# Windowed attention and a gated feed-forward on one core: the second layer of units 8 to 15 as seven half-size products

## The chip, the cores and the metric

The kernel runs on one core of one Trainium2 chip. The metric is device time in microseconds (us): the time of one execution of the program on the chip. The engines are TensorE (PE, with its weight loads as PEld), VectorE (DVE), ScalarE (ACT), GpSimd (POOL) and SyncE (SP), which here issues the DMA transfers.

## What is computed

```python
# q, k, v: 8 x 8 heads x 576 x 64
scores = q @ k.T / sqrt(64)          # heads 0-3: the last 32 positions; heads 4-7: every 4th of the last 128
attn   = softmax(where(mask, scores, -1e9))
x      = (attn @ v), heads side by side   # 4608 tokens x 512
h      = x @ w_in                     # 512 -> 2048
g      = h * tanh(softplus(h))        # Mish
out    = g @ w_out                    # 2048 -> 512
```

The weights come as 64-bit floats and everything is single precision. The kernel keeps that precision by splitting numbers into a high and a low half-precision part and multiplying high x high, high x low and low x high.

## The kernel before

The 4608 tokens are worked through in 16 units of 288 tokens (`HT`), each half of one batch entry. A unit has four pairs of heads: pairs 0 and 1 attend to a plain window, pairs 2 and 3 to the dilated one. Units 0 to 2 run the attention in fp32 with transposes on TensorE ("direct"); units 3 to 15 run it in split half precision, with transposes by DMA.

The order of everything is written out by hand in the list `ORDER`: each word is one step of one unit (or of a piece of the weights), and a step that yields is continued when its name comes again. The names that matter here: `wl`, `wm`, `ws`, `ww`, `wp` load a piece of the weights (512 KB transfers), take its magnitudes, find its scale, build single-precision words out of the 64-bit ones (`w_words`, L406 to L409: a shift, then two passes on VectorE) and split them (`w_split`). `pr` (`prep`) scales q, k and v of a unit: VectorE reduces the magnitudes of q, k and v (L306), a small product spreads the bound over the partitions (L313), and the split parts follow. `sp`, `sc`, `ex`, `tp`, `va`, `tx` are the scores of a pair, their maximum and subtraction, the exponentials, the transposes, the product with v and the transposes of x. `ff` (`ff1`, L862) is the first layer for 256 of the 2048 hidden columns, ending in Mish on ScalarE (L867). `gt` (`gate`, L883 and L885) splits a chunk of 512 hidden columns: ScalarE writes the high part, VectorE the low part. `fo` (`ff2`, L895) is a quarter of the second layer for one of four blocks of 128 outputs: 12 products (4 blocks of 128 of the contraction by three split terms). After the fourth quarter ScalarE scales the block out of PSUM (L909) and SyncE stores it. `kw` issues products of zeros (L924).

```python
seq = [(1, 0, k) for k in range(FPC)] + [(0, i, k) for k in range(FPC) for i in (1, 0)]
for n, (wi, gi, k) in enumerate(seq):
    nc.tensor.matmul(po[:, :HT], w2[:, e, j, wi, k * P:(k + 1) * P], d["g"][j][:, gi, k, :], ...)
```

PSUM is four tiles `b` of two banks; the digit behind "=" in the list says which one a step takes. Every product with a new weight block has its own weight load.

Of the kernel before, what the change touches and what calls it, by code (L numbers as in the profile page):

```python
# [10 lines left out]
F16 = mybir.dt.float16  # L11
BF16 = mybir.dt.bfloat16
F32 = mybir.dt.float32
I32 = mybir.dt.int32
I64 = mybir.dt.int64
# [10 lines left out]
SUM_EXP = 14  # L26
TINY = 2.0 ** -40
EXP_BITS = 0x7F800000
P_SCALE = 2.0 ** 14
G_SHIFT = 2.0 ** -14  # L30
# [19 lines left out]
tx1.0 wp0.1.1 ww0.2.0 ff0.1=3 tx1.3 wl1.3.0 tx1.2 ff0.1 tx1.3 wp0.2.1 tx1.2 tx1.3 ff1.0=1 wl1.2.0 sp2.3=2 ff1.1=0  # L50
wl1.3.1 gt0.3=0 ff0.1 ff1.0 fs1 pr2 ff1.2=3 ff1.1 ff1.2 gt0.3 sc2.3 wm1.3.0 gt0.0=1 wp0.2.0 ww1.3.0 wm1.2.0 ww1.3.0
wp0.2.0 ff1.0 pr2=1 ff1.1 tp2.0=0 pr2 wm1.3.1 ww1.3.1 gt0.0 sp2.1=1 tp2.0 ff0.2=0 ff0.2 ff1.2 ww1.3.1 wl1.2.1 cs2
ff1.6=3 ww1.2.0 ex2.3 sc2.1 ws1.3=2 ff1.6 wm1.2.1 ws1.3 ex2.1 ff0.2 ww1.2.1 ff1.3=2 ff1.3 ws1.2=1 ww1.2.0 ws1.2 ff1.3
gt1.0=2 tp2.3=0 sp2.2=2 wp1.3.1 wp1.3.1 tp2.3 wp1.2.0 gt1.1=3 gt1.0 ff1.6 ff1.4=1 ww1.2.1 gt1.1 ff1.4 ld3 pr3 ff0.3=0
ff0.3 ff1.5=3 wp1.2.0 ff0.3 va2.3=0 wp1.3.0 pr3 ff1.5 ff1.4 wp1.2.1 va2.3 wl1.0.0 ff1.7=1 ff1.7 va2.3 sc2.2 pr3
wl1.0.1 wp1.2.1 ff1.5 gt1.2=4 tp2.1=3 gt1.2 ff1.7 va2.0=0 tp2.1 wm1.0.0 ww1.0.0 wp1.3.0 va2.0 wl1.1.1 ex2.2 ff0.5=1
ff0.5 va2.0 ff0.4=3 ff0.4 pr3 tp2.2=2 wm1.0.1 wl1.1.0 fo1.2.0=0 fo1.2.1 ff0.4 ww1.0.1 ff0.5 tx2.0=3 tp2.2 tx2.0
ww1.0.0 tx2.0 tx2.3=1 tx2.3 wm1.1.0 va2.1=2 fo1.2.2 tx2.3 va2.2=3 ww1.0.1 va2.1 va2.1 va2.2 fo1.3.0 fo1.3.1 tx2.1=1
va2.2 pr3=2 wm1.1.1 fs2 gt0.1=5 tx2.1 tx2.2=3 ww1.1.0 fo1.3.2 tx2.2 tx2.2 tx2.2 tx2.1 pr3 ww1.1.1 ws1.0=2 fo0.2.0=3
gt0.1 ws1.0 tx2.1 gt1.3=6 wp1.0.0 ws1.1=1 fo0.2.1 gt0.2=7 ww1.1.1 wp1.0.1 ws1.1 ww1.1.0 wp1.0.0 wp1.1.1 fo0.3.0  # L60
wp1.1.0 wp1.1.1 ff2.1=2 wp1.1.0 ff2.0=1 wp1.0.1 gt1.3 ff2.0 ol xa3 ff2.1 ff2.0 pr3 ff2.1 gt0.2 pr3 pr3 pr3 pr3 fo0.3.1
# [921 lines left out]
```

## Time and profile before

| | |
|---|---|
| median of 3 runs | 902.95 us (902.22 to 905.34) |
| profiled execution | 906.53 us, its span 904.8 us |
| TensorE busy | 892.1 us (99%) |
| VectorE, ScalarE, GpSimd busy | 605.2, 569.0, 18.7 us |
| mean granted clock of TensorE | 0.992 of full speed |
| second layer (L895) | 392.9 us busy in 3072 products |
| first layer (L862) | 390.3 us busy in 3072 products |

An engine's busy time is the union of its instructions' spans. Products are pipelined: the span of one holds its way through the array, so neighbours overlap, and the pace of a group is read from the starts of the group and of the one behind it. In the timeline a row gives start, length, engine, line, operation, output and inputs, shape and count, and in brackets the idle time before it.

### The profile page before, as it was taken

To read this page: it belongs to the slowest core of one execution; us is meant where nothing else is said; L and a number is where in the kernel's file an instruction comes from. 1 tells how busy PE (TensorE), PEld (TensorE's weight loads), DVE (VectorE), ACT (ScalarE), POOL (GpSimd) and SP (SyncE) were. 2 spreads that over 40 slices of the span, in tenths; PEclk is the share of its full clock that TensorE was granted. 3 is DMA by queue.
4 is the path that set the end of the run, shared out by engine and by line. 5 is a ranking of instruction groups with operands and counts; after the bars stand their busy time and mean duration, and the time that the engine had idled before them with its cause. 6 is when DMAs were issued, how large, how long until landed. Compare 5 with 4: busy or idle time off the path is not lost.

```text
span 904.8 us, 21327 instructions
## 1 busy us (share of the span) xinstructions
PE 892.1 (99%) x9181; PEld 722.7 (80%) x9184; DVE 605.2 (67%) x893; ACT 569.0 (63%) x827; POOL 18.7 (2%) x92
## 2 busy tenths in 40 slices
PE   8989999999999999999999999999999999999998
PEld 7868888778878888888888888888888888888776
DVE  4888989798998867767487686878656453722120
ACT  4678887485865856867584765868546845553141
POOL 1000002100000000000000000000000000000000
PEclk9899999999999999999999999999999999999999
DMA  7863440235445544332524435264053132141010
GB/s 241 233 244 107 141 144 12 86 95 119 120 119 127 105 77 124 86 70 72 115 56 109 80 72 116 61 133 99 16 105 96 28 63 50 33 71 29 7 34 27
DMA packets 161711, 84.20 MB, mean 93 GB/s; under 512 B 127312, under 2 KB 157520, under 8 KB 161616
## 3 DMA queue, kind: packets, MB, share of 16 engines
q1 hardware_dynamic: 161616, 82.84, 38.5%
q8 instruction: 72, 1.18, 0.5%
q14 instruction: 23, 0.19, 0.1%
HBM read 49.02 MB, written 9.44 MB: 65 GB/s over the span
## 4 chain that ended last, share of the span: by engine, by line
PE 92%; DVE 3%; SPq 2%; DMA 2%; issue 0%; ACT 0%; DVEq 0%; ACTq 0%
PE b L895 42%; PE b L862 40%; PE b L768 4%; PE b L620 3%; PE b L762 2%; PE b L924 1%; DMA raw<-in_w_out 1%; DVE w L422 1%; SPq L469 1%; DMA vn<-in_v 1%; SPq L471 0%; DVE raw L409 0%; PE b L739 0%; PE b L376 0%; DVE raw L408 0%
## 5 line engine op out<-in xcount | busy, mean ns | idle before, releaser
L895 PE MATMUL b<-g,w 128*128 128x288 f16 x3072 | 392.9, 286 | 0.0
L862 PE MATMUL b<-x,w 128*128 128x288 f16 x3072 | 390.3, 286 | 0.5 <-ACT pp L748 0.5
L862 PEld LDWEIGHTS <-w 128*128 128x128 f16 x3072 | 298.1, 98 | 75.8 <-issue 0.7
L895 PEld LDWEIGHTS <-w 128*128 128x128 f16 x3072 | 296.2, 98 | 74.1
L867 ACT ACTIVATE hm<-b,fs 128x576 f32<-128x576 f32 x128 | 93.1, 738 | 130.8 <-PE b L862 128.4
L885 DVE SCALAR_TENSOR_TENSOR g<-hm,sg,g 128x1152 f16<-128x1152 f32 x64 | 89.4, 1409 | 65.5 <-ACT g L883 65.5
L909 ACT ACTIVATE y<-b,fo 128x288 f32<-128x288 f32 x60 | 43.3, 736 | 62.9 <-PE b L895 55.8
L883 ACT ACTIVATE g<-hm,sg 128x1152 f16<-128x1152 f32 x64 | 79.0, 1243 | 3.7 <-PE b L895 3.4
L782 DVE RECIPROCAL rec<-den 72x8 f32<-72x8 f32 (+1 forms) x64 | 12.0, 188 | 73.0 <-ACT den L778 68.4
L691 ACT ACTIVATE sb<-sb,ln_p 96x768 f32<-96x768 f32 (+3 forms) x52 | 46.3, 895 | 14.6 <-DVE sb L652 14.3
L652 DVE TENSOR_TENSOR sb<-sb,nm 96x512 f32<-96x512 f32 (+4 forms) x64 | 49.2, 768 | 2.2
L650 DVE TENSOR_REDUCE nm<-sb 96x4 f32<-96x512 f32 (+4 forms) x64 | 48.8, 763 | 1.8
L783 DVE TENSOR_TENSOR xs<-b,rec 72x512 f32<-72x512 f32 (+1 forms) x64 | 39.7, 620 | 6.3
L867 ACT ACT_TABLE_LOAD x33 | 42.3, 1283 | 0.6
L644 DVE SCALAR_TENSOR_TENSOR sb<-b,sc,m_r 96x768 f32<-96x768 f32 (+1 forms) x26 | 25.4, 977 | 21.1 <-PE b L620 21.1
L691 ACT ACT_TABLE_LOAD x30 | 38.5, 1283 | 0.5
L532 ACT ACTIVATE qn<-qn,s 128x1152 f32<-128x1152 f32 x13 | 16.3, 1252 | 35.4 <-DVE s L302 35.4
L644 DVE SCALAR_TENSOR_TENSOR sb<-b,sc,m_d 72x832 f32<-72x832 f32 (+1 forms) x26 | 24.8, 954 | 19.1 <-PE b L620 19.1
L778 ACT ACTIVATE den<-b 96x6 f32<-96x6 f32 (+1 forms) x52 | 8.8, 170 | 40.0 <-PE b L768 38.9
L620 PEld LDWEIGHTS <-q 64*72 64x72 f16 (+1 forms) x1092 | 27.2, 116 | 6.4 <-issue 5.5
L729 DVE TENSOR_TENSOR p<-sb,p 96x768 f16<-96x768 f32 (+3 forms) x35 | 31.1, 894 | 0.0
L620 PE MATMUL b<-k,q 64*72 64x104 f16 (+3 forms) x1092 | 30.9, 210 | 0.0
(139 smaller groups left out, 822.1 us busy)
## 6 DMA issues: line engine op xcount, KB each, us to landing
qn<-in_qT SPq DMA_DIRECT2D x16, 576.0 KB
out_T<-y SPq DMA_DIRECT2D x64, 144.0 KB
raw<-in_w_in SPq DMA_DIRECT2D x16, 512.0 KB
raw<-in_w_out SPq DMA_DIRECT2D x16, 512.0 KB
vn<-in_v SPq DMA_DIRECT2D x48, 128.0 KB
vdn<-in_vd SPq DMA_DIRECT2D x32, 104.0 KB
knd<-in_kdT SPq DMA_DIRECT2D x16, 208.0 KB
knp<-in_kT SPq DMA_DIRECT2D x8, 320.0 KB
```

Of the source, the lines that this page charges most:

```text
L620: nc.tensor.matmul(o, q, k, start=start, stop=stop, skip_group_check=True)
L644: nc.vector.scalar_tensor_tensor(args[0], args[1], d["sc"][:nq], args[2], ALU.mult, ALU.add)
L650: nc.vector.tensor_reduce(nm[:nq, :, j:j + n], x, axis=AX.X, op=ALU.max, negate=True)
L652: nc.vector.tensor_tensor(blocked(sb, c0, n, w), x, nm[:nq, :, j:j + n].unsqueeze(3).broadcast_to([nq, 2, n, w]), op=ALU.add)
L691: nc.scalar.activation(x, x, AF.Exp, bias=ln_p[:nq])
L783: nc.vector.tensor_tensor(xs[:nq, :nb].rearrange("p j (h e) -> p h j e", h=2), avv[:, :, :, :D], rc.unsqueeze(3).broadcast_to([nq, 2, nb, ...
L862: nc.tensor.matmul(ph[:, h, :HT], w1[j][:, c, wi, k * P:(k + 1) * P], x_of(d, xi, c), start=(n == 0), stop=(n == len(seq) - 1))
L867: nc.scalar.activation(d["m"][j][:, k0:k0 + 2], ph[:, :, :HT], AF.Mish, scale=d["fs"][:, j:j + 1])
L883: nc.scalar.activation(g[:, 0], m, AF.Identity, scale=sg)
L885: nc.vector.scalar_tensor_tensor(g[:, 1], m, sg, g[:, 0], ALU.mult, ALU.subtract)
L895: nc.tensor.matmul(po[:, :HT], w2[:, e, j, wi, k * P:(k + 1) * P], d["g"][j][:, gi, k, :], start=(j == 0 and n == 0), stop=(j == NCH - 1 a ...
L909: nc.scalar.activation(o, src, AF.Identity, scale=fo)
```

## The change

The second layer of units 8 to 15 (`SEVENS`) is no longer one product of 512 outputs x 2048 hidden columns x 288 tokens but a Strassen scheme of Winograd's form: both factors and the result are cut into 2 x 2 quarters, and seven products of half the size in each direction are formed. Four of the weights' quarters enter as they are, three sums of weights are formed once (`w_sums`, in small steps while units 3 to 8 run) and kept in half-precision pairs; four sums of a unit's hidden values are formed in place for each half of the contraction (`gate_sums`), and seven quarters are split into parts (`gate_of`). For the sums all quarters must share one scale, so `rescale` brings the output weights to one scale, and the gates of all chunks use one factor (`g_1`, `sg` of width 1).

The three accumulators x, y, z of a unit lie side by side in one PSUM tile, and are read while later products still add to them; the last unit has them in three tiles. The outputs are stored as two blocks of 256 rows.

```diff
+    def gate_of(u, p, n):
...
+            src = m[:, :, :, :HF] if n in (0, 2) else m[:, :, :, HF:]
+        nc.scalar.activation(hi, src, AF.Identity, scale=sg)
+        yield
+        nc.vector.scalar_tensor_tensor(lo, src, sg, hi, ALU.mult, ALU.subtract)
+
+    def gate_sums(u, p):
+
+        b11, b12, b21, b22 = quarters(U[u]["m"][p])
+        for a, b, op in ((b22, b12, ALU.subtract), (b12, b11, ALU.subtract), (b11, b22, ALU.add), (b21, b11, ALU.subtract)):
+            nc.vector.tensor_tensor(a, a, b, op=op)
+            yield
+
+    PRODUCTS = (("11", 0, 0, 0), ("12", 0, 1, 2), (0, 3, 0, 1), (1, 2, 0, 0), (2, 3, 1, 0), (3, 1, 0, 1), ("22", 2, 1, 0))
+
+    def product(u, n, p):
...
+        acc = [d["po"][acc][:, e, acc * HF:(acc + 1) * HF] for e in range(2)]
...
+        for e in range(2):
+            for q, (wi, gi, k) in enumerate(seq):
+                nc.tensor.matmul(acc[e], left(l, e, p, wi)[:, k * P:(k + 1) * P], right(gi, k),
...
+            nc.scalar.activation(into(half, t), by(acc), AF.Identity, scale=fo)
...
+                nc.vector.scalar_tensor_tensor(o, by(acc)[:, e], fo, o, ALU.mult, ALU.add)
```

A row of `PRODUCTS` names the left factor, the split of the right one, its place in it and the accumulator. A step `fq8.3.0` is the first half of the contraction of the fourth product of unit 8: 2 x 12 products of 144 columns (`HF`).

The bounds of q and k come from ScalarE, as sums of magnitudes over a row instead of maxima, and are spread with an fp32 transpose and an fp32 product instead of one bf16 product:

```diff
-            amax(m[:, 2 + i:3 + i], x)
+            magnitudes(m[:, 2 + i:3 + i], x)
...
+            nc.scalar.activation(t, x, AF.Abs, scale=0.5, accum_out=o[:n])
...
-        mr = yield from over_partitions(m, 6)
+        mr = yield from tops_of(m, 6)
```

The conversion of the weights loses its shift pass on VectorE; GpSimd prepares the low words, and takes the magnitudes of the output weights over from ScalarE:

```diff
-            nc.vector.tensor_scalar(a[:, c], a[:, c], 3, None, ALU.logical_shift_left)
-            yield
-            nc.vector.scalar_tensor_tensor(lo[:, c], lo[:, c], 29, a[:, c], ALU.logical_shift_right, ALU.bitwise_or)
-            nc.vector.scalar_tensor_tensor(lo[:, c], hi[:, c], -0x80000000, lo[:, c], ALU.bitwise_and, ALU.bitwise_or)
+            nc.gpsimd.tensor_scalar(lo[:, c], lo[:, c].bitcast(U32), LOW_SCALE, LOW_BIAS, ALU.mult, ALU.add)
+            yield
+            nc.vector.scalar_tensor_tensor(a[:, c], a[:, c], 3, lo[:, c], ALU.logical_shift_left, ALU.bitwise_or)
+            yield
+            nc.vector.scalar_tensor_tensor(lo[:, c], hi[:, c], -0x80000000, a[:, c], ALU.bitwise_and, ALU.bitwise_or)
             yield
```

The room for the weights' sums is taken from buffers: x has two instead of three, q2 and k2 of a unit one instead of two, the scores three instead of four, and the spare buffers of the DMA transposes go. `ORDER` is a new list throughout. It has 143 products of zeros where there were 239, and most of the attention of unit 1 stands before the first step of the first layer.

The order of the instructions shows three places. On TensorE, in the second layer of unit 8, one quarter of a block ends and the next begins; `g_99` and `g_100` are the split gates, `w_92` is the output weights. Before:

```order
L895 LDWEIGHTS w_92
L895 MATMUL b_71<-g_99,w_92 128x288
L895 LDWEIGHTS w_92
L895 MATMUL b_71<-g_100,w_92 128x288
L895 LDWEIGHTS w_92
```

After the change, in the same layer, the fourth product ends (a sum of weights kept in `g_105`) and the fifth begins (kept in `g_106`); `b_70` is the tile of the three accumulators:

```order
L1062 LDWEIGHTS g_105
L1062 MATMUL b_70<-g_101,g_105 128x144
L1062 LDWEIGHTS g_106
L1062 MATMUL b_70<-g_99,g_106 128x144 [waits Activation_49]
L1062 LDWEIGHTS g_106
```

The products are half as wide, each still behind a load of its own, and the first one behind a read of the accumulator waits for ScalarE.

On VectorE, gates of a unit in the middle of units 8 to 15. Before, two gates' low parts stand between bounds (L306) and attention:

```order
L564 SCALAR_TENSOR_TENSOR vh<-vn,s,vh 128x12x64 [waits Activation_49]
L564 SCALAR_TENSOR_TENSOR vdh<-vdn,s,vdh 104x16x64 [waits Activation_49]
L801 TENSOR_TENSOR g_104<-xs,g_104 72x512 [waits DMAHW6_49,Activation_49]
L306 TENSOR_REDUCE m<-knd 128x1 [waits DMAHW2_49,DMAHW1_49]
L885 SCALAR_TENSOR_TENSOR g_97<-hm,sg,g_97 128x1152 [waits Activation_49]
L885 SCALAR_TENSOR_TENSOR g_98<-hm,sg,g_98 128x1152
L306 TENSOR_REDUCE m<-vn 128x1 [waits DMAHW4_49,DMAHW3_49,DMAHW2_49]
L306 TENSOR_REDUCE m<-vdn 72x1 [waits DMAHW6_49,DMAHW7_49,DMAHW5_49,DMAHW0_49]
```

After, the gates, the sums in place (`hm<-hm`) and the read-outs (`y<-b_70`) stand together, with waits for ScalarE's high part in between:

```order
L1036 SCALAR_TENSOR_TENSOR g_101<-hm,sg,g_101 128x1152 [waits Activation_49]
L1036 SCALAR_TENSOR_TENSOR g_100<-hm,sg,g_100 128x576
L1042 TENSOR_TENSOR hm<-hm 128x4x144 [waits DVE_49] x4
L1036 SCALAR_TENSOR_TENSOR g_103<-hm,sg,g_103 128x1152 [waits PE_49,Activation_49]
L1081 SCALAR_TENSOR_TENSOR y<-b_70,fo,y 128x2x72 [waits DMAHW2_49,PE_49]
L1081 SCALAR_TENSOR_TENSOR y<-b_70,fo,y 128x2x72
L1036 SCALAR_TENSOR_TENSOR g_102<-hm,sg,g_102 128x1152 [waits Activation_49]
L835 RECIPROCAL rec<-den 72x8 [waits Activation_49]
```

The bounds of k have left; a half gate, four sums and two read-outs have come, and three of the four gates wait for ScalarE.

On VectorE in the head, where the first pieces of the weights are built into words. Before, a piece takes three passes (L406, L408, L409):

```order
L406 TENSOR_SCALAR w_88<-w_88 128x1024 [waits Activation_49]
L408 SCALAR_TENSOR_TENSOR raw<-raw,w_88 128x1024 [waits DMAHW7_49,DMAHW0_49,DVE_49]
L409 SCALAR_TENSOR_TENSOR raw<-raw 128x1024 [waits DVE_49]
L782 RECIPROCAL rec<-den 96x2x3 [waits Activation_49]
L783 TENSOR_TENSOR xs<-b_71,rec 96x2x3x64 [waits DVE_49,PE_49]
L306 TENSOR_REDUCE m<-vn 128x1 [waits DMAHW5_49,DMAHW4_49,DMAHW3_49]
```

After, it takes two (L443, L445), the first of which waits for GpSimd's pass over the low words (`Pool`):

```order
L443 SCALAR_TENSOR_TENSOR w_88<-w_88,raw 128x1024 [waits DMAHW4_49,DMAHW5_49,Activation_49,Pool_49]
L443 SCALAR_TENSOR_TENSOR w_91<-w_91,raw 128x1024 [waits DMAHW6_49,DMAHW7_49,Activation_49,Pool_49]
L445 SCALAR_TENSOR_TENSOR raw<-raw,w_91 128x1024 [waits DVE_49]
L445 SCALAR_TENSOR_TENSOR raw<-raw,w_88 128x1024
L443 SCALAR_TENSOR_TENSOR w_91<-w_91,raw 128x512 [waits DMAHW0_49,Activation_49,Pool_49]
L445 SCALAR_TENSOR_TENSOR raw<-raw,w_91 128x512 [waits DVE_49]
L443 SCALAR_TENSOR_TENSOR w_91<-w_91,raw 128x512 [waits DMAHW1_49,Activation_49,Pool_49]
```

Two passes a piece are left, behind one more engine.

## Rows read from the trace of the kernel before

**Rows 1.** The page, busy us, share of the span and instructions of each engine.

```profile
PE 892.1 (99%) x9181; PEld 722.7 (80%) x9184; DVE 605.2 (67%) x893; ACT 569.0 (63%) x827; POOL 18.7 (2%) x92
```

**Rows 2.** Stretches: us, busy us (x instructions) of PE, PEld, DVE, ACT, POOL, clock, DMA.

```profile
0.00:100.00 100.00, 91.10 (x911) 75.02 (x915) 76.98 (x139) 67.72 (x128) 3.16 (x20) 0.93 0.63 194
100.00:200.00 100.00, 100.00 (x993) 81.46 (x991) 89.63 (x135) 74.28 (x105) 10.80 (x18) 1.00 0.34 100
200.00:300.00 100.00, 100.00 (x1129) 80.69 (x1128) 87.03 (x139) 68.02 (x97) 0.90 (x11) 1.00 0.48 110
...
500.00:600.00 100.00, 100.00 (x1056) 80.98 (x1055) 73.15 (x107) 67.92 (x99) 0.84 (x10) 1.00 0.41 79
...
800.00:904.80 104.80, 101.05 (x875) 80.88 (x872) 15.63 (x18) 30.82 (x44) 0.00 (x0) 0.99 0.13 30
```

**Rows 3.** The timeline of TensorE around 150 us, both layers.

```profile
142.88 6.04 PE L862 MATMUL b<-x,w 128*128 128x288 f16 x48
148.76 10.45 PE L895 MATMUL b<-g,w 128*128 128x288 f16 x84
159.05 1.14 PE L862 MATMUL b<-x,w 128*128 128x288 f16 x8
```

**Rows 4.** Groups of TensorE: busy us, mean ns of one, idle us before.

```profile
L895 PE MATMUL b<-g,w 128*128 128x288 f16 x3072 | 392.9, 286 | 0.0
...
L924 PE MATMUL b<-zeros 128*128 128x128 f16 x239 | 20.7, 260 | 5.3 <-DVE wm L380 2.5 <-DVE zeros L919 1.0 <-DVE xs L783 0.9
```

**Rows 5.** The timeline of TensorE in three places, short products.

```profile
45.62 0.72 PE L739 MATMUL b<-ident,sb 96*128 96x96 f32 x6
46.18 0.52 PE L617 MATMUL b<-m_fb,ident_b 72*72 72x416 bf16 x2
...
74.39 1.07 PE L924 MATMUL b<-zeros 128*128 128x128 f16 x16 [0.34 <-DVE xs L783]
75.30 0.42 PE L810 MATMUL b<-ident,xs 72*128 72x72 f32 x4
...
136.63 1.07 PE L376 MATMUL b<-w,ones 128*128 128x128 bf16 x16
137.56 0.65 PE L895 MATMUL b<-g,w 128*128 128x288 f16 x4
```

**Rows 6.** Groups of weight loads, the second layer's.

```profile
L895 PEld LDWEIGHTS <-w 128*128 128x128 f16 x3072 | 296.2, 98 | 74.1
```

**Rows 7.** The timeline of TensorE at 402 us, products with v.

```profile
402.73 0.90 PE L768 MATMUL b<-vdh,pT 104*128 104x65 f16 x24
403.46 1.64 PE L895 MATMUL b<-g,w 128*128 128x288 f16 x12
```

**Rows 8.** Groups of VectorE, shapes apart.

```profile
L885 DVE SCALAR_TENSOR_TENSOR g<-hm,sg,g 128x1152 f16<-128x1152 f32 x64 | 89.4, 1409 | 65.5 <-ACT g L883 65.5
...
L306 DVE TENSOR_REDUCE m<-qn 128x1 bf16<-128x1152 f32 x13 | 17.5, 1347 | 3.6 <-DMA qn<-in_qT 3.6
...
L406 DVE TENSOR_SCALAR w<-w 128x1024 int32<-128x1024 int32 x15 | 10.7, 710 | 3.7 <-ACT w L361 3.7
...
L652 DVE TENSOR_TENSOR sb<-sb,nm 72x576 f32<-72x576 f32 x12 | 9.0, 754 | 0.4
...
L306 DVE TENSOR_REDUCE m<-knd 128x1 bf16<-128x832 f32 x7 | 7.1, 1012 | 0.0
```

**Rows 9.** Groups of GpSimd, shapes apart.

```profile
L286 POOL COPY m_r<-m_r 96x384 bf16<-96x384 bf16 x1 | 1.5, 1494 | 0.0
...
L272 POOL CAST m_s<-m_f 96x352 bf16<-96x352 f32 x1 | 0.5, 472 | 0.0
```

**Rows 10.** Groups of ScalarE, shapes apart.

```profile
L883 ACT ACTIVATE g<-hm,sg 128x1152 f16<-128x1152 f32 x64 | 79.0, 1243 | 3.7 <-PE b L895 3.4
L909 ACT ACTIVATE y<-b,fo 128x288 f32<-128x288 f32 x60 | 43.3, 736 | 62.9 <-PE b L895 55.8 <-issue 3.9 <-DVE s L302 1.4
```

**Rows 11.** The timeline at the end, the last read-out.

```profile
901.13 0.77 ACT L909 ACTIVATE y<-b,fo 128x288 f32<-128x288 f32 x1 [0.69 <-PE b L895]
```

More of the change, by code (lines that the diff above doesn't have):

```diff
@@ L174 @@
 BY_BLOCK = {(0, 3, 0)}
+SUMS_BY_POOL = False
 QB = 96
@@ L216, in attn_mish_ffn_kernel @@
     DIRECT = 3
+    SEVENS = range(8,16)
+    BY_POOL = {(1, g) for g in range(NCH)}
+    HF = HT // 2
     WIDE = 2
@@ L330, in top_of, with tops_of @@
         return o
+    def tops_of(m, n):
+        pm = take("b", banks)[:, 0]
+        nc.tensor.transpose(pm[:n, :P], m, ident)
+        yield
+        c = small.tile([n, n + 1], F32, name="cd", bufs=2)
+        nc.vector.tensor_reduce(c[:, :1], pm[:n, :P], axis=AX.X, op=ALU.max)
+        nc.vector.tensor_scalar(c[:, 1:], ident[:n, :n], c[:, :1], None, ALU.mult)
+        yield
+        o = pm[:, 256:256 + n]
+        nc.tensor.matmul(o, ones[:n].broadcast_to([n, P]), c[:, 1:], start=True, stop=True)
+        yield
+        return o
     raws, ready = {}, {}
@@ L705, in open_late @@
             nc.gpsimd.memset(pTs[-1], 0.0)
+        late_sums = late.tile([P, 12 * CH], F16, name="late_sums")
         x16s.append(late.tile([QB, 2 * NR * P], F16, name="x16"))
@@ new lines, in w_sums, with put, tt @@
+    def w_sums(e):
+        add, sub = ALU.add, ALU.subtract
+        eng = nc.gpsimd if SUMS_BY_POOL else nc.vector
+        t = take("gl", gs[:NCH + 1]).rearrange("p i k t -> p (i k t)")[:, :4 * CH].bitcast(F32).rearrange("p (j n) -> p j n", j=2)
+        pair = lambda n, i: w2[:, e + n[0], n[1]:n[1] + 2, i]
+        a11, a12, a21, a22 = (0, 0), (0, 2), (2, 0), (2, 2)
+        def put(n):
+            for j in range(2):
+                nc.scalar.copy(left(n, e, j, 0), t[:, j])
+            yield
+            for j in range(2):
+                nc.vector.tensor_tensor(left(n, e, j, 1), t[:, j], left(n, e, j, 0), op=sub)
+            yield
+        def tt(a, b, op):
+            eng.tensor_tensor(t, a, b, op=op)
+        tt(pair(a11, 0), pair(a21, 0), sub)
+        tt(t, pair(a11, 1), add)
+        yield
+        tt(t, pair(a21, 1), sub)
+        yield
+        yield from put(2)
+        tt(pair(a21, 0), pair(a22, 0), add)
+        tt(t, pair(a21, 1), add)
+        yield
+        tt(t, pair(a22, 1), add)
+        yield
+        yield from put(0)
+        tt(t, pair(a11, 0), sub)
+        yield
+        tt(t, pair(a11, 1), sub)
+        yield
+        yield from put(1)
+        tt(pair(a12, 0), t, sub)
+        yield
+        tt(t, pair(a12, 1), add)
+        yield
+        yield from put(3)
```

454 lines of the change are left out of this document (285 added, 169 removed).

## The prediction

> **What bounds the kernel now.** I read the busy times first, then the table of stretches, then single stretches of the timeline. TensorE is busy for 892.1 of 904.8 us [rows 1], and the stretches show where the rest is [rows 2]: from 100 to 800 us it has no gap at all; it misses 8.9 us in the first 100 us (91.10 busy) and 3.75 us after 800 us, which is the last output's way out. A stretch in which TensorE is 100% busy may still be padded, so I checked the pace: 84 products of 288 columns start at 148.76 us and the next group at 159.05 us, 122.5 ns each, and 48 from 142.88 to 148.76 us, again 122.5 ns [rows 3]. 288 columns at 2.4 GHz are 120 ns. So the kernel is a dense row of products, and only less work for TensorE, or less lost in the head, can shorten it. The listed mean of 286 ns of one product [rows 4] is its latency; the pace has to be read from starts. The head also holds 20.7 us of products of zeros that keep the clock up [rows 4].
>
> VectorE is the second engine: 87 to 90% busy between 100 and 300 us, 73% between 500 and 600 us, 16 of the last 105 us [rows 2]. At 89.63% it held TensorE up for nothing [rows 2], which I use below as the load that is known to be harmless.
>
> **The second layer of units 8 to 15.** Before, a unit issues 4 x 4 x 12 = 192 products of 288 columns; half of that layer is 1536 x 122.5 ns = 188.2 us. After, it is 7 products x 2 x 2 x 12 = 336 of 144 columns a unit, 2688 in all, each with its own weight load. No row has 144 columns, so I take the pace from both sides: 16 products of 128 columns, each with a load of 128 x 128 weights, go from 74.39 to 75.30 us, 56.9 ns each, and 16 others from 136.63 to 137.56 us, 58.1 ns each [rows 5]. On the lines from these to 122.5 ns at 288 columns, 144 columns cost 63.5 and 64.5 ns; if the 2.5 ns that 288 columns take over 120 ns stay as they are, 62.5 ns. I take 63.5 ns: 170.7 us, **-17.5 us** (-20.2 to -14.8). The load itself lasts 98 ns [rows 6], longer than that, so the question is whether it holds the pace. Against it: 24 products of 65 columns, each with its own 128 weights to a row, go from 402.73 to 403.46 us, 30.4 ns each [rows 7]. Loads of 98 ns overlap there at a third of their length.
>
> The Trainium skill says otherwise ("TensorE: Matmul & The Clock Gate", section "Back-to-back issue gap"): a sustained stream of load and product pairs runs at about 81 ns a product at 128 columns. By that figure the seven products would cost at least 2688 x 81 = 218 us, an estimate from that page, and the change would lose about 30 us on this term and end near 932 us. This trace does not agree at 128 columns, but its runs of such products are short, and what the page describes is kept as rival 1.
>
> **The filler.** The new list has 143 zero products for 239. The 96 that go cost 56.9 ns each [rows 5]: **-5.5 us**, if the idle time of the head doesn't grow in their place.
>
> **The weights' conversion.** The shift is now merged into one of the two remaining VectorE passes and the low words are made on GpSimd; VectorE loses 16 x 710 ns = 11.4 us [rows 8]. VectorE is busy 76.98 of the first 100 us [rows 2], so not all of it is on the path, and the same list runs most of the attention of unit 1 before the first product of the first layer. I count **-2 us**. Ends: -9 us (nearly all the idle time of the head) and +10 us: GpSimd gets 15 + 2 passes over the low words and 8 over the output weights. Its cast of 352 elements took 472 ns, so 1024 take 1.4 us; its copy of 384 took 1494 ns, which would make 4.0 us [rows 9]. At 1.4 us the passes are hidden behind the loads; at 4.0 us the four pieces of which the first layer's first product has need come 4 x 2.6 = 10 us later.
>
> **The bounds of q and k.** For each of 13 units, 1347 ns for q's 1152 elements and, by 1012 ns for 832, some 1.6 us for k's 1152 to 1472 leave VectorE, 38 us in all [rows 8]. ScalarE gets the same passes; at 1243 ns for 1152 elements [rows 10] that is about 37 us on 569 [rows 1], and it stays behind VectorE. TensorE instead of one product of 6 columns now does an fp32 transpose of 128 columns and an fp32 product of 6. Six fp32 transposes of 96 columns take 0.56 us (45.62 to 46.18 us [rows 5]), so 128 columns are 0.12 us; the small product I bound by nothing and the same again. 13 x 0.2 = **+2.5 us** (1 to 5, twice that).
>
> **The gates and sums.** A unit of 8 to 15 has 6 full and 2 half gates for 4 full ones, 8 sums of 576 elements and 6 read-outs of 144 on VectorE. With 1409 ns a gate, half of it for the half one, 0.75 us a sum (a subtraction of 576 elements took 754 ns) [rows 8] and half of ScalarE's 736 ns for a read-out of 288 [rows 10], that is 2.8 + 1.4 + 6.0 + 2.2 = 12.4 us, less 2.9 us of bounds: 9.5 us net, of a unit's 50 us. Between 500 and 600 us VectorE rises from 73 to about 90 of 97 us, 93%, a little over the 89.63% that held nothing up. The weights' sums and the rescaling (20 passes of 1024, 16 of 512, 4 of 4096 elements: 25 + 10 + 11 us by 1012 ns for 832 elements and 710 ns for 1024 [rows 8]) fall on units 3 to 8, where 16 us of bounds leave. So none of it costs TensorE time, as long as the order holds; where VectorE is late, the next thing late is the low part of a gate and with it a half-size product.
>
> The new wait is that of the accumulators: all three of a unit lie in one PSUM tile, and TensorE may not go on in it while ScalarE or VectorE reads it. The order shows that wait on the first product after a read. Five reads a unit; a read by ScalarE is 736 ns [rows 10], and behind it on ScalarE may stand a gate of 1243 ns. The list puts other products between nearly everywhere; in unit 8 after the fourth product there is none, and I find some four such places. Four times about 1 us: **+4 us** (0; 7 x 5 x 0.74 = 26 us if nothing covered them). The last unit has its accumulators apart.
>
> **The end.** Now 0.77 us of read-out and the store end it after the last product [rows 11]. Two read-outs of 144 on VectorE and a store of twice the size: **+0.5 us** (0 to 3).
>
> **Sum:** -17.5 - 5.5 - 2 + 2.5 + 4 + 0.5 = -18.0 us against the profiled execution's 906.5 us (span 904.8 us and 1.7 us around it). The median of the runs, 902.95 us, stands 3.6 us below that; I put the same difference on it: **885 us**. What this kernel's measurement can tell from no change is about 0.3%, 2.7 us.
>
> **Rivals.**
> 1. The half-size products are paced by their weight loads. For it: a load lasts 98 ns [rows 6], a product of 144 columns only some 63. Against it: 30.4 ns at 65 columns [rows 7]. At 98 ns the seven products cost 263.4 us, +75.2 instead of -17.5: 978 us. It decides from 70.2 ns a product, where the layer's 188.2 us and the other terms (-0.5) are used up. 0.05. The Trainium skill's 81 ns lie beyond that point.
> 2. The chain of a unit (gate, low part, sum in place, gate, read-out in one PSUM tile) is too tight for engines that issue in order: TensorE stands 1.5 us more in each of 8 units. For it: VectorE at 93%, one buffer fewer for x, q, k and the scores. Against it: 89.63% without a gap [rows 2]. 897 us, with half of its cases over 900. 0.18.
> 3. The head gains more: with the conversion lighter and most of unit 1 done early, 10 us more of the 29.6 us of idle time and filler go [rows 2, 4]. 875 us. 0.12.
> 4. GpSimd is slow or blocks VectorE in the head, +10 us as bounded above: 895 us. 0.05. The Trainium skill has a rule for it ("SBUF — State Buffer", section "Who interferes with whom"): a VectorE instruction with two SBUF inputs and a GpSimd one that reads SBUF exclude each other for whole instructions. No row here shows the two at once.
> That the change does not do what it says is excluded by its order: 2688 products of 144 columns, each with its load.
>
> **How the numbers follow.** The forecast (877 to 893 us) gets 0.60. All of it, of rival 3 and of rival 4, and half of rival 2, are faster by over 0.3%: 0.60 + 0.12 + 0.05 + 0.09 = 0.86. Of the rest of rival 2, 0.05 is within 0.3% and 0.04 slower; with rival 1, slower is 0.09. The range of 870 to 899 us leaves out 0.05 of rival 1, some 0.10 of rival 2 and the fastest of rival 3, 0.04.
>
> **What would show it.** The groups of half-size products at 62 to 65 ns from start to start; TensorE's gaps between 100 and 880 us under 6 us in all, each ended by ScalarE or VectorE at the half-size products; VectorE near 93% from 500 to 600 us; the first product of the first layer before 55 us and head gaps near 9 us; GpSimd passes of 1024 elements under 2 us. It is wrong if half-size products start 70 ns or more apart, or if TensorE's gaps in units 8 to 15 sum to over 15 us.

## The result, and the profile after

The changed kernel takes 895.85 us (median of 4 runs, 894.41 to 897.61) where the kernel before took 903.52 us in the same comparison: ratio 0.9915, 95% interval 0.9889 to 0.994. Measured once more with six runs it was 896.1 us (0.991, 0.9877 to 0.9943). So it is faster by 7 to 8 us, not by the 18 us that I forecast; the direction and the range held, the size did not. The profiled execution took 897.61 us, its span 895.6 us.

The page's busy times of the changed kernel answer to [rows 1], its table of stretches (columns as in [rows 2]) to those rows:

```profile
PE 875.9 (98%) x10264; PEld 741.2 (83%) x10266; DVE 706.0 (79%) x1035; ACT 621.4 (69%) x924; POOL 69.9 (8%) x117
```

```profile
0.00:100.00 100.00, 86.25 (x810) 69.72 (x813) 73.28 (x112) 65.02 (x117) 32.62 (x36) 0.91 0.63 194
100.00:200.00 100.00, 99.98 (x956) 81.19 (x955) 78.89 (x118) 69.70 (x104) 32.42 (x27) 0.99 0.29 87
...
500.00:600.00 100.00, 98.77 (x1367) 86.54 (x1365) 89.88 (x132) 79.41 (x116) 0.90 (x10) 1.00 0.36 78
...
800.00:895.60 95.60, 91.10 (x1168) 82.53 (x1166) 42.56 (x57) 37.45 (x48) 0.00 (x0) 0.99 0.14 34
```

The middle is nearly as dense as before. The surprise is the first row: TensorE executes 101 products fewer in the first 100 us and is busy 86.25 us in place of 91.10, at a granted clock of 0.91 in place of 0.93. Fewer zero products, and more idle time in their place.

The pace of the half-size products is read from starts in TensorE's timeline:

```profile
605.62 3.16 PE L1062 MATMUL b<-g,late_sums 128*128 128x144 f16 x48
608.62 0.90 PE L821 MATMUL b<-vdh,pT 104*128 104x65 f16 x24
...
612.30 3.16 PE L1062 MATMUL b<-g,w 128*128 128x144 f16 x48
615.30 0.27 PE L359 MATMUL b<-ident,m 128*6 128x128 f32 x1
```

Both groups of 48 take 3.00 us: 62.5 ns each. TensorE's waits (engine, line, what it waited for, us in total, times, longest), first in the first 100 us, then in all the rest:

```profile
PE b L415 <- DVE w L443: 3.2, 1, 3.2
PE b L412 <- DVE w L443: 3.0, 3, 1.1
PE b L815 <- DVE m L538: 2.3, 1, 2.3
PE b L335 <- DVE sb L704: 2.2, 1, 2.2
PE b L923 <- ACT den L829: 1.1, 1, 1.1
...
PE b L1062 <- ACT y L1076: 1.1, 2, 0.9
PE b L923 <- DMA x<-x: 0.3, 1, 0.3
PE b L1062 <- DVE y L1081: 0.2, 1, 0.2
```

L412 and L415 are the sums of the weights' magnitudes over the partitions, which wait for VectorE's word pass (L443); L815 is the product with v, L335 a bound. Groups (busy us, mean ns of one, idle before) that answer to [rows 4, 8, 9]:

```profile
L398 POOL TENSOR_SCALAR w<-raw 128x1024 f32<-128x1024 f32 x8 | 27.5, 3441 | 26.9 <-DMA raw<-in_w_out 26.4
...
L443 DVE SCALAR_TENSOR_TENSOR w<-w,raw 128x1024 int32<-128x1024 int32 x15 | 23.4, 1569 | 0.9 <-POOL w L398 0.7 <-ACT w L400 0.2
...
L441 POOL TENSOR_SCALAR raw<-raw 128x1024 int32<-128x1024 uint32 x15 | 19.0, 1268 | 47.9 <-DMA raw<-in_w_in 42.8 <-PE b L863 2.4 <-DVE rec L835 1.9
...
L1140 PE MATMUL b<-zeros 128*128 128x128 f16 x143 | 11.8, 252 | 1.0 <-DVE zeros L1135 1.0
...
L366 PE MATMUL b<-cd,ones 6*128 6x6 f32 x26 | 4.9, 259 | 0.0
```

**Where TensorE's time went.** I gave every interval from the start of one product to the start of the next to its program step; of an interval longer than 0.4 us, all but 0.1 us counts as idle. The sums, in us:

| | before | after | |
|---|---|---|---|
| second layer | 377.9 | 358.5 | -19.4 |
| zero products | 19.0 | 10.9 | -8.1 |
| bounds of q and k | 0.6 | 5.5 | +4.9 |
| idle before 110 us | 10.8 | 17.3 | +6.4 |
| idle after 110 us | 0.0 | 2.2 | +2.2 |
| first layer | 377.7 | 378.3 | +0.6 |
| attention, weights' scales | 113.7 | 117.6 | +3.8 |
| to the last product's start | 899.7 | 890.1 | -9.6 |

The second table is the head alone, the time lost until 150 us: zero products, idle time, and what the other products took above their usual pace ("slow"), for the profiled execution of each kernel. Of the slow time about 2.5 us stand in stretches at half clock in the kernel before, and about 8.1 us in the change. The runs below are read with this table.

| lost by 150 us | zero products | idle | slow | sum |
|---|---|---|---|---|
| before | 19.0 | 9.1 | 13.4 | 41.6 |
| the change | 10.9 | 15.9 | 17.5 | 44.3 |
| the change again | 13.1 | 13.1 | 18.1 | 44.3 |
| b1_old_list_gpsimd | 17.3 | 10.9 | 11.6 | 39.9 |
| b2_old_list_less_filler | 11.5 | 9.4 | 14.0 | 34.9 |
| b3_both_terms | 11.5 | 12.9 | 15.2 | 39.6 |
| a3_filler_in_waits | 23.5 | 6.8 | 13.4 | 43.7 |
| a4_weights_first | 12.2 | 19.1 | 19.6 | 50.9 |
| e3_no_gpsimd | 10.9 | 22.7 | 18.0 | 51.6 |

(A profile is one execution and heads differ by some us from one to the next: that of the kernel before is 3.6 us above its first median, that of b2 is 1.6 us below its own. The times below are medians. Times inside the kernel that the expectations name, 93.9 us for one, lie 0.23 us before the profile's.)

### The profile page after: what moved, and what is told of

Same layout as the page of the kernel before. It is cut to its first block, busy times and chain, and to the rows that moved or that the text cites. A ratio compares the mean times of both kernels' runs of the same rounds, so it can differ in the third digit from the quotient of the medians.

```text
span 895.6 us, 23819 instructions
## 1 busy us (share of the span) xinstructions
PE 875.9 (98%) x10264; PEld 741.2 (83%) x10266; DVE 706.0 (79%) x1035; ACT 621.4 (69%) x924; POOL 69.9 (8%) x117
## 4 chain that ended last, share of the span: by engine, by line
PE 90%; DVE 3%; DMA 2%; POOL 1%; SPq 1%; ACT 1%; issue 1%; DVEq 0%; ACTq 0%; POOLq 0%
PE b L923 39%; PE b L1111 21%; PE b L1062 18%; PE b L672 4%; PE b L821 4%; PE b L815 1%; DVE w L443 1%; POOL w L398 1%; DMA raw<-in_w_out 1%; DMA vn<-in_v 1%; DVE raw L445 1%; DVE w L454 1%; PE b L415 1%; DMA x<-x 0%; PE b L792 0%
## 5 line engine op out<-in xcount | busy, mean ns | idle before, releaser
L923 PEld LDWEIGHTS <-w 128*128 128x128 f16 x3072 | 297.8, 98 | 75.7 <-DVE w L454 1.2
L1111 PE MATMUL b<-g,w 128*128 128x288 f16 x1536 | 198.6, 286 | 0.0
L1111 PEld LDWEIGHTS <-w 128*128 128x128 f16 x1536 | 147.3, 98 | 36.9 <-issue 0.2
L1062 PE MATMUL b<-g,w 128*128 128x144 f16 x1536 | 101.2, 226 | 0.4 <-DVE y L1081 0.2
L1062 PEld LDWEIGHTS <-w 128*128 128x128 f16 x1536 | 97.6, 98 | 1.6 <-issue 0.6
L1034 ACT ACTIVATE g<-hm,sg 128x1152 f16<-128x1152 f32 (+1 forms) x64 | 71.5, 1127 | 16.9 <-PE b L1062 14.0
L1036 DVE SCALAR_TENSOR_TENSOR g<-hm,sg,g 128x1152 f16<-128x1152 f32 (+1 forms) x64 | 79.8, 1261 | 4.3 <-ACT g L1034 4.2
L743 ACT ACTIVATE sb<-sb,ln_p 96x768 f32<-96x768 f32 (+3 forms) x52 | 46.1, 893 | 10.4 <-DVE sb L704 10.3
L1042 DVE TENSOR_TENSOR hm<-hm 128x576 f32<-128x576 f32 x64 | 47.8, 754 | 2.8 <-ACT hm L929 1.8
L1013 DVE SCALAR_TENSOR_TENSOR g<-hm,sg,g 128x1152 f16<-128x1152 f32 x32 | 44.8, 1409 | 2.8 <-ACT g L1011 2.8
L836 DVE TENSOR_TENSOR xs<-b,rec 96x384 f32<-96x384 f32 (+1 forms) x64 | 39.7, 621 | 5.8
L780 ACT CAST p<-sb 96x768 f16<-96x768 f32 (+3 forms) x52 | 40.8, 790 | 2.8 <-DMA pT<-p 2.6
L1062 PE MATMUL b<-g,g 128*128 128x144 f16 x576 | 40.3, 226 | 1.1 <-ACT y L1076 1.1
```

Of the source, the lines that this page charges most:

```text
L743: nc.scalar.activation(x, x, AF.Exp, bias=ln_p[:nq])
L923: nc.tensor.matmul(ph[:, h, :HT], w1[j][:, c, wi, k * P:(k + 1) * P], x_of(d, xi, c), start=(n == 0), stop=(n == len(seq) - 1))
L1034: nc.scalar.activation(hi, src, AF.Identity, scale=sg)
L1036: nc.vector.scalar_tensor_tensor(lo, src, sg, hi, ALU.mult, ALU.subtract)
L1042: nc.vector.tensor_tensor(a, a, b, op=op)
L1062: nc.tensor.matmul(acc[e], left(l, e, p, wi)[:, k * P:(k + 1) * P], right(gi, k), start=(n in opens and p == 0 and q == 0), stop=(last and ...
```

## The experiments

My first theory (A) was that GpSimd's slow passes (3.4 us where ScalarE took 1.15) had eaten the head's gain; its rival (B) blamed the new list, which loads the weights later.

**GpSimd taken out of the conversion.** Three kernels: magnitudes back on ScalarE, low words back on VectorE, both.

```diff
-    BY_POOL = {(1, g) for g in range(NCH)}
+    BY_POOL = set()
```

```diff
-            nc.gpsimd.tensor_scalar(lo[:, c], lo[:, c].bitcast(U32), LOW_SCALE, LOW_BIAS, ALU.mult, ALU.add)
             yield
-            nc.vector.scalar_tensor_tensor(a[:, c], a[:, c], 3, lo[:, c], ALU.logical_shift_left, ALU.bitwise_or)
+            nc.vector.tensor_scalar(a[:, c], a[:, c], 3, None, ALU.logical_shift_left)
+            nc.vector.scalar_tensor_tensor(lo[:, c], lo[:, c], 29, a[:, c], ALU.logical_shift_right, ALU.bitwise_or)
...
```

> The magnitudes of the output weights go back from GpSimd (eight passes of 2.9 to 3.7 us) to ScalarE (1.15 us each). Theory A (the head's gain was lost to GpSimd's part in the weights' conversion): TensorE's 3.5 us of waiting at 93.9 us for the output weights' words and the 3.4 us at half clock behind it go, 5 us in all: ratio to the kernel before 0.986, about 891 us. Theory B (it was lost to the new list, which loads the weights later and stops ScalarE for v): the stall is moved, not removed, and the time stays within 1 us of 895.9 (ratio 0.990 to 0.993).

> The low words go back to VectorE, as in the kernel before (shift by 3 of 0.69 us, then the two passes of 1.22 us); the list and GpSimd's magnitudes stay. Theory A: the chain landing, word pass, first product gets shorter by GpSimd's pass and by the stretching of VectorE's passes (1.5 and 1.4 us mean against 1.22), but VectorE has 11 us more: 2 us less, 894 us (ratio 0.989). Theory B: the passes were not what the head waited for, and the time stays or grows by up to 3 us: 895 to 899 (0.991 to 0.995).

> Both: nothing of the weights' conversion on GpSimd, list as in the changed kernel. Theory A: 6 to 7 us less than the changed kernel, 889 us (ratio 0.984), first product of the first layer before 52 us instead of 55.7. Theory B: first product still at 54 to 57 us, time 893 to 897 (0.988 to 0.993).

Measured: 900.7 us (ratio 0.9963, 0.9946 to 0.9979), 897.92 us (0.9933, 0.9914 to 0.9952) and 904.61 us (1.0012, 0.9997 to 1.0026). Theory A falls: without GpSimd the change is about 4.7, 1.9 and 8.6 us slower (against 896.0 us, the middle of its two medians; the 1.9 us lie within the intervals), and the last is no faster than the kernel before. The waits of e1 between 60 and 125 us, ScalarE's and then TensorE's, point to the reason for its part:

```profile
ACT w L400 <- DMA raw<-in_w_out: 6.7, 1, 6.7
...
PE b L792 <- ACT hm L929: 4.4, 1, 4.4
PE b L415 <- DVE w L443: 3.2, 1, 3.2
```

The wait for the output weights' words (L415) is still there, so GpSimd's pace was not its cause. And ScalarE, which has TensorE's next inputs to make, stands 6.7 us at the head of its queue for a transfer. In the change that wait, 26.4 us in all, is GpSimd's, behind which next to nothing queues (VectorE waits 0.7 us for it): its passes are three times as long and pay.

**The prediction's two head terms by themselves,** in the kernel before and its list: the low words on GpSimd (b1), eight calls of `kw` with 96 zero products left out (b2), both (b3).

```diff
-            nc.vector.tensor_scalar(a[:, c], a[:, c], 3, None, ALU.logical_shift_left)
+            nc.gpsimd.tensor_scalar(lo[:, c], lo[:, c].bitcast(U32), LOW_SCALE, LOW_BIAS, ALU.mult, ALU.add)
+            nc.vector.scalar_tensor_tensor(a[:, c], a[:, c], 3, lo[:, c], ALU.logical_shift_left, ALU.bitwise_or)
             yield
-            nc.vector.scalar_tensor_tensor(lo[:, c], lo[:, c], 29, a[:, c], ALU.logical_shift_right, ALU.bitwise_or)
...
```

> The kernel before with one part of the change: the weights' low words are made by GpSimd, so that VectorE makes two passes per piece in place of three; its list stays. The runs e1 to e3 left 8.5 us to GpSimd's part within the new list. Theory C (the conversion's passes on VectorE and ScalarE pace the head, whatever the list): 4 to 8 us less than before, 897 to 900 us (ratio 0.991 to 0.996). Theory D (the head goes by the landing of the weights and by waits that the old list covers with zero products): within 2 us of before (0.998 to 1.002). My prediction's term for it was 2 us less, between 9 less and 10 more.

> The kernel before with 96 of its 239 zero products left out (eight of its twenty calls, all after the first 42 products), nothing else. As my prediction priced it (a zero product is TensorE's own time on the path): 5.5 to 8 us less, 896 to 899 us (ratio 0.991 to 0.994). Theory D (zero products stand in waits that stay when they go): within 1.5 us of before (0.998 to 1.002), TensorE's idle time up by as much as its zero products fall; slower by up to 3 us if the clock is granted at half speed for longer.

> The kernel before with both edits of b1 and b2: low words on GpSimd and 96 zero products less, its list otherwise. My prediction's terms: 7.5 us less, 895 to 896 us (ratio 0.992). Theory E (they are worth what they were apart: 2.4 more and 1.0 less): 904 to 906 us (1.000 to 1.003). If GpSimd's part pays only where no zero products stand in the waits it shortens: 899 to 901 us (0.995 to 0.998).

Measured: 905.29 us (1.0028, 1.0017 to 1.0039), 901.93 us (0.9987, 0.9976 to 0.9998), 904.92 us (1.0013, 0.9991 to 1.0036). The conversion cost 2.4 us instead of giving 2; the zero products gave 1.0 instead of 5.5; together 1.9 us more (interval: 0.8 less to 3.3 more) where I had 7.5 less. In b2 TensorE waits at places where zero products had stood (first 100 us; lines are 20 further down than in the kernel before: L759 are the transposes of the exponentials, L944 is `kw`). How much of the 96 products' time came back so can't be read from these two profiles, which stand on opposite sides of their medians; the medians say, all but 1.0 us:

```profile
PE b L759 <- ACT sb L709: 2.5, 1, 2.5
PE b L944 <- DVE wm L400: 1.1, 1, 1.1
...
PE b L759 <- ACT sb L705: 0.9, 1, 0.9
PE b L342 <- DVE ms L515: 0.9, 1, 0.9
```

In b1 TensorE gets two waits, 4.2 us in all, for the words of the first layer's weights (L375 sums their magnitudes; 1.2 us in the kernel before); most likely, and not shown by a run, because VectorE's pass now stands behind GpSimd's, in a list that places it for ScalarE and VectorE alone.

```profile
PE b L375 <- DVE w L409: 4.2, 2, 3.0
```

**Zero products put into the new waits,** 176 of them:

```diff
-va0.2=1 ... ws0.3=3 ... pr1=3 ... ws0.1=1 ... ws1.3=0
+kw16=1 kw16=1 va0.2=1 ... kw16=3 kw16=3 kw16=3 ws0.3=3 ... kw16=3 kw16=3 pr1=3 ... kw16=1 ws0.1=1 ... kw16=0 kw16=0 kw16=0 ws1.3=0
```

> The changed kernel with 176 more zero products, put at the five places where TensorE waits longest in the head (17.0, 34.4, 49.0, 61.8 and 93.9 us). If the waits cost by what the clock does behind them: the 6.8 us at half clock from 36.7 us and the 3.4 us from 98.1 us go, 3 to 5 us less, 891 to 893 us (ratio 0.986 to 0.989). If they cost only themselves: within 1 us of 895.9 (0.990 to 0.993). If the zero products run on the path (as my prediction priced them): 10 us more, 906 us (1.002).

Measured: 896.73 us (0.9929, 0.9908 to 0.9951), the time of the change. TensorE's busy time in the first 100 us rises from 86.25 to 93.70 us, and the time stays:

```profile
0.00:100.00 100.00, 93.70 (x982) 78.14 (x983) 71.41 (x110) 64.51 (x117) 33.83 (x36) 0.93 0.64 195
```

The second table shows it as a swap: 12.6 us more zero products, 9.1 less idle, 4.1 less slow. In this head, most of the zero products and the idle time are two names of the same waits; some 3.5 us of the added products stood outside them and used up about what the slow time gave back.

**The list's order.** In a4 the weights' loads stand in the old order and ScalarE's row sums of v behind unit 0's exponentials; a5 has only the second.

```diff
-cs0 ... lv0 pr0 sp0.3=3 ... ex0.1 wl0.0.0 lv1 ex0.1 ... wl0.0.1 ... pr0 pr0=1 wl0.3.1 tp0.3=3 wl0.3.0 ld1
+cs0 wl0.0.0 ... wl0.0.1 lv0 wl0.3.1 wl0.3.0 lv1 sp0.3=3 ... ex0.1 ex0.1 ... pr0 pr0 pr0=1 tp0.3=3 ld1
```

> The changed kernel with the loads of the head in the old order: the first weight piece ahead of v, the second with it, the other two ahead of unit 1's v, q and k; and ScalarE's row sums of v behind unit 0's exponentials, where they no longer stop it for 5.3 us. Theory B (the new list's order took the head's gain: first weights words at 16.8 us in place of 9.4, first product of the first layer at 55.7 in place of 48.7): first product 3 to 6 us earlier and as much off the time, 890 to 893 us (ratio 0.985 to 0.989). Rival: the head is paced by its attention and conversion passes, whose place in the list stays: within 1 us of 895.9 (0.990 to 0.993).

> The changed kernel with only ScalarE's row sums of v moved behind unit 0's exponentials (the second half of the run before; the loads keep the new order). If ScalarE's 5.3 us of waiting for v hold up the exponentials that TensorE waits for: 1 to 3 us less, 893 to 895 us (ratio 0.988 to 0.991). If the landing of v sets when unit 0's chain goes on: within 1 us of 895.9 (0.990 to 0.993); then the 8 us that the run before lost came from v's later landing.

Measured: 903.67 us (1.0005, 0.9989 to 1.0021) and 898.46 us (0.9949, 0.9932 to 0.9967). Theory B falls in this form too: with both edits the kernel is 7.7 us slower, 2.5 of it, within the intervals, by the row sums' place alone. TensorE's longest wait in a4's first 60 us is the transpose of v's bound (L365) for VectorE's maximum of ScalarE's row sums (L555), and ScalarE's (second row) is then for TensorE, for the scores behind it:

```profile
PE b L365 <- DVE ms L555: 4.6, 1, 4.6
...
ACT sb L751 <- PE b L745: 10.4, 3, 8.4
```

The first of these waits is 2.0 us in a5, where only the row sums are late. My reading is that v has to come early, because unit 0's chain hangs on it, and that the weights' later landing was the smaller evil.

**The bounds by one half-word product,** at the place of the transpose (e4), then at that of the fp32 product (f2).

```diff
-        mr = yield from tops_of(m, 6)
+        mb = pool.tile([P, 6], BF16, name="m2", bufs=2)
+        nc.vector.tensor_copy(mb, m)
+        mr = take("b", banks)[:, 0, 256:262]
+        yield
+        yield
+        nc.tensor.matmul(mr, ones_b.broadcast_to([P, P]), mb, start=True, stop=True)
+        yield
```

> The bounds of q and k for units 3 to 15: the row sums of ScalarE are copied to half words on VectorE and go over the partitions by one product of 6 columns, in place of the fp32 transpose and the fp32 product (13 x 109 ns and 26 x 155 ns, 5.5 us). Both theories: that time is TensorE's own in the middle of the kernel, where it never waits, so 4.5 to 5 us go: 891 us (ratio 0.986). If something else set the pace there, under 1.5 us go. The bounds may come out smaller by a rounding of half words.

> As e4 (bounds by one half-word product), but the product stands where the fp32 product stood in TensorE's order, two calls behind the copy, so that it does not wait 2.5 us for the copy as it did once in e4 (279.7 us). The bounds' price is then seen alone: 5 us of TensorE's time go (13 x 109 and 26 x 155 ns, less 13 half-word products): 890.5 to 891.5 us (ratio 0.985 to 0.987), if nothing in the middle takes it back; 894 to 896 (0.989 to 0.992) if a wait there does.

Measured: 895.01 us (0.9904, 0.9884 to 0.9924) and 893.47 us (0.9885, 0.9865 to 0.9905). TensorE's time for the bounds falls from 5.5 to 0.4 us in e4 and to 1.1 us in f2; e4 gives 2.2 of it back in one wait, between 100 and 892 us, which f2 does not have:

```profile
PE b L335 <- DVE m L569: 2.2, 1, 2.2
```

By f2 the new bounds cost some 2.5 us of the time (893.47 against 895.85 and 896.1; the intervals overlap) and 4.5 us of TensorE's.

**The wait at 94 us filled with work,** alone (f1) and with f2's bounds (f3):

```diff
-ww1.3.0 ws1.3=0 gt1.0=2 ww1.2.1 gt1.3=3 ws1.3 ... wp1.2.1 ff1.2 ff0.3=0 ff0.3 ff1.5=3
+ww1.3.0 ff1.2 ff0.3=0 ws1.3=3 gt1.0=2 ww1.2.1 gt1.3=3 ff0.3 ws1.3 ... wp1.2.1 ff1.5=3
```

> The changed kernel with the sums over the partitions of output weights 3 and 2 put behind 36 products of the first layer in TensorE's order (5 us of work that was behind them), where TensorE waited 3.5 us at 93.9 us for their words. If that wait is one that other work can fill: it shrinks to under 1 us and the time falls by 2.5 to 4 us, 892 to 893.5 us (ratio 0.987 to 0.989). If the head's length is set by the chain load, words, scale, split (so that the wait comes back at the next group): within 1 us of 895.9 (0.990 to 0.993).

> f1 and f2 together. If both gains are real and apart: 7 to 9 us less than the changed kernel, 887 to 889 us (ratio 0.981 to 0.984).

Measured: 897.43 us (0.9925, 0.9905 to 0.9945) and 890.66 us (0.9849, 0.9825 to 0.9872). In f1 the wait itself (its line is L436 there) shrinks from 3.2 to 0.8 us, and the time does not:

```profile
PE b L436 <- DVE w L464: 0.8, 2, 0.5
```

f3 is the fastest kernel of the study, 13 us under the kernel before and 5 under the change. That f1's edit helps only beside f2's (2.8 us, with intervals that overlap) is not explained.

**The change without its products,** three times: units 8 to 15 by whole products at the places of the half-size ones. g1 takes the groups of outputs one after the other, g2 with other distances, g3 two at a time.

```diff
-gq10.0.0=1 gq10.0.0 ... fq10.0.0=0 ... fq10.0.1 ... fq10.6.1
+gt10.0 gt10.2 gt10.0 gt10.2 ... fo10.0.0=0 ... fo10.0.2 ... fo10.3.3
```

> The changed kernel without its products: units 8 to 15 take the second layer by the ordinary 16 groups of 12 whole products each, put at the places of the half-size ones, the sums of the weights (units 5 to 7) and of the gates fall away with them; the list's head, the conversion on GpSimd and the bounds by row sums stay. Theory E (the products' 18.4 us came whole into the end time, and all the rest of the change costs 8 to 11 us): 912 to 915 us, slower than the kernel before (ratio 1.008 to 1.013). Rival F (the rest is worth something, and part of the products' gain was lost in waits of the middle): 899 to 907 us (0.995 to 1.004).

> As g1, with the whole products of units 8 to 15 spread otherwise over the same places: the third group of outputs starts one place after the read-out of the second, since in g1 TensorE waited there 15 times for ScalarE's read-out of the bank it had just filled (14.3 us in all, 20.0 us of idle time in the middle in place of the changed kernel's 2.2). Leaves out the sums of weights and gates as g1 does. Theory E: with that idle time gone 912 to 917 us (ratio 1.009 to 1.015). Rival F (part of the products' gain was lost in waits of the middle): 899 to 907 us (0.995 to 1.004). If the waits stay at the new places, over 920 us, and the run tells nothing more than g1.

> As g1 and g2 (no half-size products, no sums of weights and gates), with two groups of outputs taken side by side in the two halves of a bank, so that neither waits for the other's read-out: in g2 TensorE still waited there (11.5 us for the read-outs, 17.0 us idle in the middle). Subtracting the idle time of the middle above the changed kernel's 2.2 us gives 915 us from g1 and 919 us from g2. Theory E: this kernel comes at 912 to 919 us by itself (ratio 1.009 to 1.017), with under 7 us idle in the middle. Rival F: 899 to 907 us (0.995 to 1.004).

Measured: 933.0 us (1.0322, 1.0274 to 1.037), 933.41 us (1.0323, 1.0295 to 1.035) and 934.72 us (1.0347, 1.0316 to 1.0378). All three form the 3072 whole products of the second layer; what they put out is not the layer's result, so only their times are used. As clean controls they fail: TensorE idles 20.0, 17.0 and 16.9 us after the head. In g1 it is one wait (500 to 930 us), that for the bank that is still read out:

```profile
PE b L1122 <- ACT y L1136: 14.3, 15, 1.5
```

By subtraction the books close: in g1 the second layer takes 377.9 us again, 19.4 more than in the change, idle time after the head 17.8 more, and 896 + 19.4 + 17.8 is 933. That the rest of the change costs some 12 us without the products (915 us, against 903 before) is therefore worked out, not shown by a run at that time.

## Why the prediction was wrong, and where right

**Second layer, -17.5 us: right.** 62.5 ns a half-size product where I took 63.5, and 19.4 us less in TensorE's books. Rival 1 is out: loads of 98 ns don't pace products of 62.5 ns that follow each other 48 at a time. The 81 ns at 128 columns of the Trainium skill ("TensorE: Matmul & The Clock Gate", section "Back-to-back issue gap") are contradicted by 62.5 ns at 144 columns; the measurement decides.

**The filler, -5.5 us: the step that failed.** I priced 96 zero products at 56.9 ns as TensorE's own time, with the proviso "if the idle time of the head doesn't grow in their place". It grew. In the change the zero products take 8.1 us less, the idle time before 110 us is 6.4 us longer, and the slow time at half clock, for which I had no term, rises from about 2.5 to 8.1 us. b2 measured the term alone at 1.0 us (0.2 to 2.2), and its runs have a mean granted clock of 0.992 where the kernel before has 0.998 beside them (medians of 10 and 22 runs). The row that could have told me was before my eyes: the zero products stood at waits for VectorE's sums [rows 4], and a product put into a wait takes no time that its removal gives back.

**The conversion, -2 us: failed too,** in its sign in the old list (b1: +2.4 us). I had counted VectorE's 11.4 us as the price. Within the new list GpSimd's part is worth 8.6 us (e3), and without it the change would have gained nothing (904.61 us); for the magnitudes, e1's waits point to the queue that stands in front of a transfer.

**The two together** were forecast at -7.5 us and measured at +1.9 (b3, -0.8 to +3.3): 9.4 of the 10.3 us by which the forecast missed. The two profiled executions agree: the head loses 41.6 us before and 44.3 after, +2.7 where I had -7.5. With the bounds (+4.9 for +2.5), the second layer (-19.4 for -17.5) and the waits (+2.2 for +4), that is 8.9 of the 9.1 us by which these two executions (906.53 and 897.61 us) miss the forecast. Rival 3, a head that gains more, did not happen.

The new list's head loses 4.7 us more than b3's (44.3 against 39.6 us by 150 us, one execution each); its waits are spread over v, the first weights' words and the output weights' words, and neither earlier loads (a4), nor later row sums (a5), nor filler (a3), nor filling the longest of them with work (f1) shortened the kernel by itself. What exactly paces this head stays open. The clock is a rival that no run decides: the median run has a mean granted clock of 0.996 before (87 runs) and 0.990 with the change (ten), and among the runs of either kernel 0.01 less goes with some 4 to 6 us more. By that slope 0.006 are 2.5 to 3.5 us, an estimate in which the waits that go with a low clock are counted too. a3, at 0.9965, takes as long as the change, but some 3.5 us of its zero products stood outside the waits.

**The bounds, +2.5 us:** about right in time (f2: 2.5), too small in TensorE's own: a transpose of 109 ns and two passes of 155 ns are 0.42 us a unit, not 0.2.

**The accumulators' waits, +4 us: right in kind, too high.** By the profile's waits TensorE stood 1.3 us for read-outs in units 8 to 15 (2.2 us idle in the first table, which counts all that an interval takes over 0.1 us), the longest at 539.6 us in unit 8, behind the fourth product, the place I had named; rival 2 did not happen. VectorE rose to 89.88% between 500 and 600 us, forecast 93, and held TensorE up for 0.2 us.

**The end, +0.5 us: right;** 4.4 us from the last product's start to the end, before 4.0.

**Rival 4** had the right sight and the wrong price. GpSimd's word pass took 1268 ns (estimated 1.4 us), its magnitudes 3441 (bounded by 4.0). VectorE's pass beside it is stretched to a mean of 1569 ns; with nothing of the conversion on GpSimd (e3) passes of that shape take 1226. It costs VectorE some 5 us (15 x 0.34) and the kernel nothing that e2 or e3 could give back. The Trainium skill's rule that the two contend ("SBUF — State Buffer", section "Who interferes with whom") agrees with that in kind. That one is held out for the whole of the other's instruction doesn't show here: the pass at 88.39 us runs for 2.02 us, and ends, inside a GpSimd pass from 87.33 to 91.05 us, as far as GpSimd's spans can be trusted.

**Of the signs that I had named,** three did not come: the first product of the first layer starts at 55.7 us (before 55), TensorE is idle for 13.8 of the first 100 us (near 9), and GpSimd's magnitudes take 3.4 us (under 2). One of the four gaps of the middle, 0.3 us, waits for a transfer at the first layer.

## What to carry to other kernels

Price filler by the wait it stands in, not by its length: remove it and the wait is left. Before a term of the head is added to a sum, book the lost time (filler, idle, half clock) up to the point where the engine runs dense, and ask what would move that sum. A slow, idle engine is a good place for work that must wait for a transfer, because nobody queues behind it; and an order written for one distribution of the work can be the wrong place to judge another.

## What the runs showed of the hardware

A multiplication of 1024 fp32 values a partition took GpSimd 3441 ns; the integer pass of the same length, multiply and add with conversion, 1268 ns. TensorE's granted clock fell to its lower level (1.2 of 2.4 GHz) in the head of the change three times: from 19.86 us, as in the kernel before from 19.40 us; from 36.93 us, in the second of two waits for VectorE (1.1 and 0.9 us) that began behind 34.6 us; and from 98.37 us, behind the wait of 3.2 us that ended at 97.64 us. In the kernel before it fell twice, the second time from 60.36 us for 3.41 us (columns: stretch, us, PE busy, clock, DMA):

```profile
19.86:30.10 10.24, 10.24 (x74) 0.50 0.99 372
36.93:43.75 6.82, 6.25 (x30) 0.50 0.02 5
98.37:101.78 3.41, 3.41 (x29) 0.50 0.00 0
```

Zero products in the waits (a3) took 4.1 us off the slow time and did not pay. That the chain which TensorE waits for sets the time there, and not the clock, is my reading and not shown; no run took the clock alone away.
